# Residual stored in the output and completed by accumulating DMA in the down stage; eight VectorE sums moved one tile later

## The chip, the cores and the metric

One core of a Trainium2 chip. The metric is device time in microseconds (us) of the whole program; smaller is better. All executions told here count as fast, and the granted TensorE clock of a profiled one is given where it was not 1.0 (within 0.001). Engines: PE is TensorE's matmuls, PEld its weight loads, DVE is VectorE, ACT is ScalarE, POOL is GpSimd, SP is SyncE, which here issues DMAs only.

## The reference

```python
x = A_x                                             # 2048 x 1024, bf16
h = x + _A_ref(_layernorm(x, axis=-1), A_wqkv, A_wo)        # linear attention, 32 heads
h2 = h + _B_ref(_layernorm(h, axis=-1), B_W_gate, B_W_up, B_W_down)   # gated ReLU, F = 3584
```

`h` is needed twice: normalized for the second half, and as the residual added to the result. The second half's product is small beside it: the norm of h2 - h is 0.0023 of the norm of h2. The comparison with the reference therefore says little of the down product.

## The kernel before

Every large product is done by a scheme with seven block products in place of eight (operands are sums of blocks, made on VectorE). The program runs through k/v products, the q products and attention (to about 288 us), the gate and up products (288 to 602 us), and the down product (602 us to the end). Three parts matter here.

(1) The end of the attention stage, per tile `t` of 128 tokens. The residual `x` is loaded into `x_res` (three buffers), the attention product is added to it on VectorE, and the result `h` is stored to DRAM and normalized. Tiles 0 to 7 of `order` are processed while the last q products run, tiles 8 to 15 while the first gate/up products run:

```python
def x_in():
    x_sb = bwork.tile([P, D], BF16, tag="x_res", bufs=XB, name="x_res")        # XB = 3
    nc.sync.dma_start(out=x_sb[:], in_=xf[t * P:(t + 1) * P, :])
...
def wo_h(borrow):
    ...
    for j in range(2):
        ...   # 8 matmuls into ps ("attn")
        with tc.high_priority():
            added[t] = nc.vector.scalar_tensor_tensor(out=h_sb[:, j * NW:(j + 1) * NW], in0=ps[:], ...)
    nc.sync.dma_start(out=h_dram[i][s][:, r // P, :], in_=h_sb[:])
    ...   # ScalarE: square, Ln, Exp, normalize -> hn
def hn_T():
    nc.sync.dma_start_transpose(out=hnT[s][i][:, :, r:r + P], in_=st["hn"][:])
```

(2) VectorE is the place of several other things at that time: `phi_end` of the last q products, and the weight sums (tg, tu) of the first gate/up products, whose place is given by a scheduling constraint.

```python
def phi_end(dst, e):
    nc.scalar.activation(out=e, in_=dst, func=ACT.Exp, bias=negb[:, 0:1], scale=1.0)
    nc.vector.tensor_scalar(out=e, in0=e, scalar1=1.0, scalar2=PHI_EPS, op0=ALU.min, op1=ALU.add)   # the clamp
    nc.vector.tensor_tensor(out=dst, in0=dst, in1=e, op=ALU.max)
...
with tc.issue_after(added[order[STS - 1]].ins):     # STS = 8: after tile 7's last add
    late_sums.pop()()                               # 4 sums tg, 4 sums tu
```

(3) The down stage. The output has four quadrants (token half i, column half j). `put` finishes a piece of one: VectorE adds the accumulator and a partial result, adds `h` (loaded again from DRAM), and ScalarE's queue stores it:

```python
def load_h(k, s):
    if k in outs:
        i, j = outs[k]
        v = dpool.tile([P, NT, DW], BF16, tag="h", bufs=3, name="h")
        nc.scalar.dma_start(out=v[:], in_=h_dram[i][s][:, :, j * DW:(j + 1) * DW])
        hres[k, s] = v

def put(k, s, ts, cs, ps, m, with_h=True, eng=nc.scalar):
    ...
    add(out=ov, in0=ps, in1=m, op=ALU.add)
    if with_h:
        add(out=ov, in0=ov, in1=hres[k, s][:, ts, cs], op=ALU.add)
    t0 = (i * HS + s * SW) // P
    eng.dma_start(out=out_v[:, t0 + ts.start:..., j * DW + cs.start:...], in_=ov)
```

Of the kernel before, what the change touches and what calls it, by code (L numbers as in the profile page):

```python
# [8 lines left out]
ALU = mybir.AluOpType  # L9
FP32 = mybir.dt.float32  # L10
BF16 = mybir.dt.bfloat16
# [20 lines left out]
def block_kernel(ctx: ExitStack, tc: tile.TileContext, x, wqkv, wo, wg, wu, wd, out, H: int):  # L32
    nc = tc.nc
    P = 128
    xf = x.flatten_outer_dims()
    of = out.flatten_outer_dims()
    S, D = xf.shape
# [6 lines left out]
    NW = 512  # L44
    NDW = P + HPC
    SW = 512
    NS = S // (2 * SW)
    KH = KC // 2
    FH = FC // 2
    HS = S // 2  # L50
    NT = SW // P
    DW = D // 2
# [15 lines left out]
    nc.gpsimd.memset(deps[:], DEN_EPS)  # L68

    dram = ctx.enter_context(tc.tile_pool(name="dram", bufs=1, space=bass.MemoryType.DRAM))  # L70
    h_dram = [[dram.tile([P, NT, D], BF16, name=f"h_dram{i}_{s}") for s in range(NS)] for i in range(2)]
    GP = 2
    NE = 2 * GP
    FQ = FH // 2
# [146 lines left out]
    order = [(i * HS + s * SW) // P + tt for s in range(NS) for i in range(2) for tt in range(NT)]  # L221
# [6 lines left out]
    with ExitStack() as actx:  # L228
# [208 lines left out]
        for c in range(KC):  # L437
            bnk, i = divmod(c, GPB)
# [72 lines left out]
    held, added, squared = [], {}, {}  # L511

    def attn_stages(t):

        i, r = divmod(t * P, HS)
        s, r = divmod(r, SW)
        st = {}

        def nd():
            o_sb = bwork.tile([P, D], BF16, tag="o_sb", name="o_sb")  # L520
            st["o"] = o_sb
            held.append(o_sb)
            ov = o_sb[:].rearrange("p (k h e) -> p k h e", k=KC, h=HPC)
            for c0, n in pieces:
                ps = ndpool.tile([P, NW], FP32, tag="ab", name="nd")
                for c in range(c0, c0 + n):
                    nc.tensor.matmul(ps[:, (c - c0) * NDW:(c - c0 + 1) * NDW], lhsT=pqT[:, c, t * P:(t + 1) * P],
                                     rhs=kvz[:, c, :], start=True, stop=True)
                ndv = ps[:, 0:n * NDW].rearrange("p (k w) -> p k w", w=NDW)
                den = bsmall.tile([P, GPB, HPC], FP32, tag="den", name="den")  # L530
                nc.scalar.activation(out=den[:, 0:n], in_=ndv[:, :, P:NDW], func=ACT.Ln, bias=deps[:], scale=1.0)
                rd = bsmall.tile([P, GPB, HPC], FP32, tag="rd", name="rd")
                nc.scalar.activation(out=rd[:, 0:n], in_=den[:, 0:n], func=ACT.Exp, scale=-1.0)  # L533
                nc.vector.tensor_tensor(  # L534
                    out=ov[:, c0:c0 + n], in0=ndv[:, :, 0:P].rearrange("p k (h e) -> p k h e", h=HPC),
                    in1=rd[:, 0:n, :].unsqueeze(3).to_broadcast([P, n, HPC, Dh]), op=ALU.mult)

        def oT():
            oT = bwork.tile([P, D], BF16, tag="oT", bufs=XB, name="oT")
            st["oT"] = oT[:].rearrange("p (c t) -> p c t", c=KC)  # L540
            nc.sync.dma_start_transpose(out=st["oT"], in_=st["o"][:])

        def x_in():
            x_sb = bwork.tile([P, D], BF16, tag="x_res", bufs=XB, name="x_res")
            nc.sync.dma_start(out=x_sb[:], in_=xf[t * P:(t + 1) * P, :])
            st["x"] = x_sb

        def wo_h(borrow):
            h_sb = st["x"]
            tot = bsmall.tile([P, 2], FP32, tag="tot", name="tot")  # L550
            for j in range(2):
                if borrow:
                    ps = pspool.tile([P, NW], FP32, tag="E", bufs=2, name="attn")
                else:
                    ps = abpool.tile([P, NW], FP32, tag="ab", name="attn")
                for c in range(KC):
                    nc.tensor.matmul(ps[:], lhsT=st["oT"][:, c, :], rhs=wo_sb[:, c, j * NW:(j + 1) * NW],  # L557
                                     start=(c == 0), stop=(c == KC - 1))
                with tc.high_priority():
                    added[t] = nc.vector.scalar_tensor_tensor(out=h_sb[:, j * NW:(j + 1) * NW], in0=ps[:], scalar=1.0,  # L560
                                                   in1=h_sb[:, j * NW:(j + 1) * NW], op0=ALU.mult, op1=ALU.add,
                                                   accum_out=tot[:, j:j + 1])
            nc.sync.dma_start(out=h_dram[i][s][:, r // P, :], in_=h_sb[:])
            st["hn"] = bwork.tile([P, D], BF16, tag="hn", bufs=HB, name="hn")

            sm = bsmall.tile([P, 6], FP32, tag="sm", name="sm")
            nmean, var, lnv, rstd, nmr = (sm[:, i:i + 1] for i in range(5))
            nc.vector.tensor_scalar(out=nmean, in0=tot[:, 0:1], scalar1=tot[:, 1:2], scalar2=-1.0 / D,
                                    op0=ALU.add, op1=ALU.mult)
            squared[t] = nc.scalar.activation(out=st["hn"][:], in_=h_sb[:], func=ACT.Square, bias=nmean, scale=1.0, accum_out=var)  # L570
            nc.scalar.activation(out=lnv, in_=var, func=ACT.Ln, bias=LN_EPS, scale=1.0 / D)
            nc.scalar.activation(out=rstd, in_=lnv, func=ACT.Exp, scale=-0.5)
            nc.scalar.activation(out=nmr, in_=nmean, func=ACT.Identity, scale=rstd)
            nc.scalar.activation(out=st["hn"][:], in_=h_sb[:], func=ACT.Identity, bias=nmr, scale=rstd)

        def hn_T():
            nc.sync.dma_start_transpose(out=hnT[s][i][:, :, r:r + P], in_=st["hn"][:])

        return nd, oT, x_in, wo_h, hn_T

    LAG = (0, 1, 1, 2, 4)
    STS = ST // NS
# [4 lines left out]
    def attn_step(step):  # L587
        for k in range(len(LAG)):
            n = step - LAG[k]
            if n in begin_at:  # L590
                n = begin_at.index(n)
                if k == 3:
                    stages[n][k](QSTEPS <= step < STS + LAG[-1])
                else:
                    stages[n][k]()
                if k == len(LAG) - 1 and n % STS >= NT:
                    left_sums(hnT[n // STS], hns[n // STS], slice(n % NT * P, (n % NT + 1) * P), nc.vector)
# [177 lines left out]
    for step in range(QSTEPS + 2, ready):  # L775
        if step == QSTEPS + 2:
            flow.pop(0)()
        attn_step(step)
    with tc.issue_after(added[order[STS - 1]].ins):
        late_sums.pop()()  # L780
    steps = QSTEPS + STS + LAG[-1] - ready
    for n in range(steps):
# [19 lines left out]
    def acc(tag):  # L802
        return accs.tile([P, 2 * NW], FP32, tag=tag, bufs=2 if tag == "A" else 1, name="acc" + tag)
# [59 lines left out]
    OUTER = (1, 2, 6, 5, 3, 7, 4)  # L863
    INNER = (2, 6, 5, 3, 4)
    outs = {2: (0, 0), 7: (1, 1), 3: (0, 1), 4: (1, 0)}
# [56 lines left out]
    prv, k = None, 0  # L922
    for r, (wt, f, fi, toks) in enumerate(runs):
        w = [ops() for _, ops in now]
        later = []
        for n, s in enumerate(toks):
# [51 lines left out]
            if k == nwin - 3:  # L978
                for x in range(2):
                    t = wpools[1].tile([P, KC * 2 * GP * P], BF16, tag=("wg", "wu")[x], name="wd")  # L980
# [16 lines left out]
    for n in range(2):  # L997
        t = fpool.tile([P, 4 * D], BF16, tag="wraw", bufs=2, name="xd")
# [19 lines left out]
    dpool = ctx.enter_context(tc.tile_pool(name="dpool", **reuse))  # L1018
# [89 lines left out]
    out_v = of.rearrange("(t p) d -> p t d", p=P)  # L1108
    hres = {}

    def load_h(k, s):

        if k in outs:
            i, j = outs[k]
            v = dpool.tile([P, NT, DW], BF16, tag="h", bufs=3, name="h")
            nc.scalar.dma_start(out=v[:], in_=h_dram[i][s][:, :, j * DW:(j + 1) * DW])
            hres[k, s] = v

    def put(k, s, ts, cs, ps, m, with_h=True, eng=nc.scalar):

        i, j = outs[k]
        o = dpool.tile([P, NT * HW], BF16, tag="o", bufs=4, name="o")
        ov = o[:, 0:(ts.stop - ts.start) * (cs.stop - cs.start)].rearrange("p (t d) -> p t d", t=ts.stop - ts.start)
        add(out=ov, in0=ps, in1=m, op=ALU.add)
        if with_h:
            add(out=ov, in0=ov, in1=hres[k, s][:, ts, cs], op=ALU.add)
        t0 = (i * HS + s * SW) // P
        eng.dma_start(out=out_v[:, t0 + ts.start:t0 + ts.stop, j * DW + cs.start:j * DW + cs.stop], in_=ov)

    def cols(j):  # L1130
        return slice(j * HW, (j + 1) * HW)
# [111 lines left out]
    for n in range(1, len(OUTER)):  # L1243
# [73 lines left out]
        else:  # L1317
            pss = []
            for p in range(4):
                ps = acc(("A", "A", "XY"[(n + 1) % 2], "XY"[n % 2])[p])  # L1320
# [12 lines left out]
                s, t0 = divmod(2 * p, NT)  # L1333
                ts = slice(t0, t0 + 2)
                v = ps[:].rearrange("p (t d) -> p t d", t=2)
# [9 lines left out]
@with_exitstack  # L1345
def kernel(
    ctx: ExitStack,
    tc: tile.TileContext,
    A_x: bass.AP,
    A_wqkv: bass.AP,  # L1350
    A_wo: bass.AP,
    B_x: bass.AP,
    B_W_gate: bass.AP,
    B_W_up: bass.AP,
    B_W_down: bass.AP,
    out: bass.AP,
):
    block_kernel(tc, A_x, A_wqkv, A_wo, B_W_gate, B_W_up, B_W_down, out, H=32)
# [30 lines left out]
```

## Time and profile before

| | us |
|---|---|
| time, median of 3 runs | 738.58 (737.89 to 739.36) |
| span in the trace | 737.3 |
| PE busy | 724.7 (98%) |
| VectorE busy | 563.8 (76%) |
| PE idle between 210 and 220 us | 1.81 |

The page's first part, busy time of each engine (share of the span, count of instructions), kernel before:

```profile
PE 724.7 (98%) x4020; PEld 382.1 (52%) x4020; DVE 563.8 (76%) x992; ACT 322.4 (44%) x580; POOL 5.6 (1%) x44
```

Busy time of each engine in two stretches (stretch, its length, then busy us and instructions of PE, PEld, DVE, ACT and POOL in this order, granted clock, share of the DMA engines, GB/s):

```profile
210.00:220.00 10.00, 8.19 (x49) 4.02 (x48) 9.89 (x30) 8.55 (x28) 0.00 (x0) 1.00 0.69 129
620.00:640.00 20.00, 20.00 (x186) 17.93 (x184) 19.73 (x18) 0.00 (x0) 0.00 (x0) 1.00 0.88 315
```

From 620 to 640 us, in the down stage, PE never idles, with VectorE almost full beside it; PE has no idle time from 500 us to its last matmul. In 210 to 220 us it is VectorE that is full, and PE idles. What PE waited for in the whole run (waiting instruction, releaser: us in total, times, longest), without the waits of the first 100 us:

```profile
PE attn L557 <- DVE x_res L560: 1.3, 1, 1.3
PE attn L557 <- DVE o_sb L534: 1.1, 4, 0.5
PE nd L527 <- DVE o_sb L534: 0.5, 1, 0.5
```

VectorE's instructions in order of time there (start, length, line, output and inputs, count). L636 to L642 are the moved sums, L217 is the clamp, L560 is the add into x_res; the one at 211.99 is tile 8's first:

```profile
208.63 0.42 DVE L636 TENSOR_TENSOR tg<-wg 128x512 f16<-128x512 bf16 x1
208.97 0.42 DVE L641 TENSOR_TENSOR tg<-wg 128x512 f16<-128x512 bf16 x1
...
210.98 0.42 DVE L642 TENSOR_TENSOR tg<-wg,tg 128x512 f16<-128x512 bf16 x1
211.32 0.42 DVE L636 TENSOR_TENSOR tu<-wu 128x512 f16<-128x512 bf16 x1
211.65 0.42 DVE L217 TENSOR_SCALAR e<-e 128x1024 bf16<-128x1024 bf16 x1
211.99 0.68 DVE L560 SCALAR_TENSOR_TENSOR x_res<-attn,x_res 128x512 bf16<-128x512 f32 x1
```

And ScalarE's exponential that the clamp at 211.65 reads. It ends at 211.08:

```profile
209.94 1.14 ACT L216 ACTIVATE e<-pq_mem,negb 128x1024 bf16<-128x1024 bf16 x1
```

### The profile page before, as it was taken

How to read it: one execution, taken by the hardware profiler on the slowest of the kernel's cores; microseconds unless marked ns; L12 is line 12 of the kernel's file. 1: busy time of each engine (PE TensorE's matmuls, PEld its weight loads, DVE VectorE, ACT ScalarE, POOL GpSimd, SP SyncE). 2: the span in 40 equal slices, each digit the busy share in tenths (PEclk: the TensorE clock that was granted, in tenths of full speed). 3: DMA queues.
4: the chain of work that ended last, by engine and by line, in shares of the span. 5: the costliest groups of instructions: out<-in, count | busy, mean ns of one | idle time of the engine just before them, and what ended most of it. 6: DMA issues, size and time to landing. Idle time of an engine off the chain costs nothing.

```text
span 737.3 us, 10605 instructions
## 1 busy us (share of the span) xinstructions
PE 724.7 (98%) x4020; PEld 382.1 (52%) x4020; DVE 563.8 (76%) x992; ACT 322.4 (44%) x580; POOL 5.6 (1%) x44
## 2 busy tenths in 40 slices
PE   7999999999999999999999999999999999999997
PEld 3444555444444444444444444444444468888666
DVE  6997644677788777688768787887786379996797
ACT  4876553778887654444344444443444120000000
POOL 1000000000000000000000000000000000000000
PEclk9999999999999999999999999999999999999999
DMA  9765002079977526175638358575483499987822
GB/s 315 159 151 159 1 1 85 31 159 222 221 172 179 128 73 207 43 207 136 196 103 243 114 187 272 185 218 195 158 284 116 140 396 335 333 288 296 295 81 78
DMA packets 146594, 132.02 MB, mean 179 GB/s; under 512 B 50928, under 2 KB 128112, under 8 KB 146544
## 3 DMA queue, kind: packets, MB, share of 16 engines
q1 hardware_dynamic: 135536, 123.30, 55.8%
q10 hardware_dynamic: 11008, 8.06, 3.4%
q8 instruction: 31, 0.51, 0.3%
q14 instruction: 19, 0.16, 0.1%
HBM read 79.95 MB, written 39.85 MB: 162 GB/s over the span
## 4 chain that ended last, share of the span: by engine, by line
PE 82%; DVE 8%; DMA 5%; ACT 4%; issue 1%; SPq 0%; DVEq 0%; POOL 0%; ACTq 0%
PE accA L828 22%; PE accY L828 8%; PE accX L828 8%; PE accA L1160 8%; PE attn L557 5%; PE Aq L314 3%; PE accA L989 3%; PE accX L1160 3%; PE Aq L454 3%; PE accY L1160 2%; PE Aq L729 2%; PE Eq L314 2%; PE accY L989 2%; PE accX L989 2%; PE Eq L454 1%; PE Eq L729 1%
## 5 line engine op out<-in xcount | busy, mean ns | idle before, releaser
L838 ACT ACTIVATE gu<-gu 128x512 bf16<-128x512 bf16 x72 | 45.4, 630 | 131.2 <-DVE gu L837 131.2
L833 ACT COPY snap<-accA 128x1024 f32<-128x1024 f32 x72 | 72.5, 1008 | 36.5 <-PE accA L828 36.4
L557 PE MATMUL attn<-wo_mem,oT 128*128 128x512 bf16 x256 | 58.7, 379 | 2.7 <-DVE x_res L560 1.3
L828 PEld LDWEIGHTS <-tu 128*128 128x128 f16 x384 | 37.6, 98 | 45.3
L828 PEld LDWEIGHTS <-tg 128*128 128x128 f16 x384 | 37.6, 98 | 45.3
L837 DVE TENSOR_TENSOR gu<-accY,snap 128x1024 bf16<-128x1024 f32 x36 | 43.9, 1219 | 10.0 <-ACT snap L833 10.0
L828 PE MATMUL accA<-hn,tg 128*128 128x512 f16 (+1 forms) x192 | 49.3, 379 | 0.0
L828 PE MATMUL accA<-hn,tu 128*128 128x512 f16 (+1 forms) x192 | 49.3, 379 | 0.0
L837 DVE TENSOR_TENSOR gu<-accX,snap 128x1024 bf16<-128x1024 f32 x36 | 43.9, 1219 | 6.4 <-PE accX L828 3.7
L154 ACT COPY u<-Aq 128x512 f32<-128x512 f32 x54 | 31.3, 582 | 36.0 <-PE Aq L314 19.3
L1160 PEld LDWEIGHTS <-x 128*128 128x128 f16 (+1 forms) x448 | 43.9, 98 | 5.5
L828 PEld LDWEIGHTS <-wu 128*128 128x128 bf16 x288 | 28.2, 98 | 34.0
L828 PEld LDWEIGHTS <-wg 128*128 128x128 bf16 x288 | 28.2, 98 | 34.0
L557 PEld LDWEIGHTS <-oT 128*128 128x128 bf16 x256 | 24.7, 98 | 33.0 <-issue 4.9
L841 DVE TENSOR_TENSOR hq<-gu 128x512 bf16<-128x512 bf16 x48 | 20.3, 423 | 14.3 <-ACT gu L838 14.2
L314 PEld LDWEIGHTS <-xT 128*128 128x128 bf16 (+1 forms) x192 | 18.6, 98 | 23.7 <-issue 2.3
L534 DVE TENSOR_TENSOR o_sb<-nd,rd 128x384 bf16<-128x384 f32 (+1 forms) x48 | 23.2, 508 | 8.8 <-ACT rd L533 6.6
L1160 PEld LDWEIGHTS <-xs 128*128 128x128 f16 x280 | 27.4, 98 | 3.2
L560 DVE SCALAR_TENSOR_TENSOR x_res<-attn,x_res 128x512 bf16<-128x512 f32 x32 | 22.0, 686 | 8.4 <-PE attn L557 8.2
L989 PEld LDWEIGHTS <-x 128*128 128x128 bf16 (+1 forms) x168 | 16.4, 98 | 19.6
L1166 DVE TENSOR_TENSOR snap<-accA,u 128x1024 f32<-128x1024 f32 x16 | 19.5, 1220 | 8.3 <-PE accA L1160 8.1
L828 PE MATMUL accA<-hs,tg 128*128 128x512 f16 x96 | 24.6, 379 | 0.0
(234 smaller groups left out, 1406.1 us busy)
## 6 DMA issues: line engine op xcount, KB each, us to landing
x<-x_dram SPq DMA_DIRECT2D x17, 896.0 KB, 8.3
x_dram<-hq SPq DMA_DIRECT2D x28, 512.0 KB, 3.2
wg<-in_B_W_gate_dram SPq DMA_DIRECT2D x14, 512.0 KB, 5.2
wu<-in_B_W_up_dram SPq DMA_DIRECT2D x14, 512.0 KB, 7.3
wraw<-in_B_W_down_dram SPq DMA_DIRECT2D x14, 512.0 KB, 5.0
x_dram<-hq SPq DMA_DIRECT2D x28, 256.0 KB, 2.6
t_dram<-wt SPq DMA_DIRECT2D x28, 256.0 KB, 2.2
xd<-x_dram SPq DMA_DIRECT2D x6, 896.0 KB, 7.2
```

The source lines that it names most:

```text
L154: copies[nm, v] = nc.scalar.copy(out=snaps[nm, v], in_=bank[v][:])
L314: nc.tensor.matmul(ps[:], lhsT=left[m - 1][:, kc, r + v * P:r + (v + 1) * P], rhs=right[m - 1][:, kc, :], start=(start and kc == 0), stop= ...
L454: nc.tensor.matmul(ps[:], lhsT=rq[m - 1][:, kc, (c + v) * P:(c + v + 1) * P], rhs=left[m - 1][:, kc, :], start=(start and kc == 0), stop=( ...
L534: nc.vector.tensor_tensor(out=ov[:, c0:c0 + n], in0=ndv[:, :, 0:P].rearrange("p k (h e) -> p k h e", h=HPC), in1=rd[:, 0:n, :].unsqueeze(3 ...
L557: nc.tensor.matmul(ps[:], lhsT=st["oT"][:, c, :], rhs=wo_sb[:, c, j * NW:(j + 1) * NW], start=(c == 0), stop=(c == KC - 1))
L729: nc.tensor.matmul(ps[:], lhsT=w(v, m)[:, kc, :], rhs=left[m - 1][:, kc, :], start=(start and kc == 0), stop=(kc == KH - 1), skip_group_ch ...
L828: nc.tensor.matmul(ps[:, v, :], lhsT=w[v][n - 1][:, kc, :], rhs=left[n - 1][:, kc, :], start=(t is not None and kc == 0), stop=(kc == KH - ...
L833: nc.scalar.copy(out=st[nm][:], in_=halves(st["A"]))
L837: add(out=g[:], in0=halves(st[nm]), in1=st[base][:], op=ALU.add)
L838: nc.scalar.activation(out=g[:, 0, :], in_=g[:, 0, :], func=ACT.Relu)
L989: nc.tensor.matmul(ps[:, t * NW:(t + 1) * NW], lhsT=x_tile(n, s, kh)[:, f, (t0 + t) * P:(t0 + t + 1) * P], rhs=w_tile(n, kh)[:, f, :], sta ...
L1160: nc.tensor.matmul(pv[:, tt, :], lhsT=left(m)[:, f, tt * P:(tt + 1) * P], rhs=right(m)[:, f, :], start=(t is not None and f == 0 and tt % ...
```

## The change

Its intent: relieve VectorE and the DMA queues in the down stage, by letting the DMA engines do the addition of h. `h` goes to the output itself, except the quadrant that is finished last; for the other three `put` adds its piece to DRAM with an accumulating DMA, which GpSimd issues. And the eight weight sums are to start behind tile 8's first add, which PE waits for.

```diff
-    h_dram = [[dram.tile([P, NT, D], BF16, ...) for s in range(NS)] for i in range(2)]
+    h_dram = [dram.tile([P, NT, DW], BF16, name=f"h_dram{s}") for s in range(NS)]
 ...
-                    added[t] = nc.vector.scalar_tensor_tensor(
+                    added[t, j] = nc.vector.scalar_tensor_tensor(
 ...
-            nc.sync.dma_start(out=h_dram[i][s][:, r // P, :], in_=h_sb[:])
+            if i == 0:
+                nc.sync.dma_start(out=of[t * P:(t + 1) * P, :], in_=h_sb[:])
+            else:
+                nc.sync.dma_start(out=h_dram[s][:, r // P, :], in_=h_sb[:, 0:DW])
+                nc.sync.dma_start(out=of[t * P:(t + 1) * P, DW:D], in_=h_sb[:, DW:D])
 ...
-    with tc.issue_after(added[order[STS - 1]].ins):
+    with tc.issue_after(added[order[STS], 0].ins):
         late_sums.pop()()
 ...
-        if k in outs:
-            i, j = outs[k]
-            v = dpool.tile([P, NT, DW], BF16, tag="h", bufs=3, name="h")
-            nc.scalar.dma_start(out=v[:], in_=h_dram[i][s][:, :, j * DW:(j + 1) * DW])
+        if k == OUTER[-1]:
+            v = dpool.tile([P, NT, DW], BF16, tag="h", bufs=2, name="h")
+            nc.scalar.dma_start(out=v[:], in_=h_dram[s][:])
 ...
         add(out=ov, in0=ps, in1=m, op=ALU.add)
+        dst = out_v[...]
+        if k != OUTER[-1]:
+            nc.gpsimd.dma_start(out=dst, in_=ov, accum_op=ALU.add)
+            return
         if with_h:
             add(out=ov, in0=ov, in1=hres[k, s][:, ts, cs], op=ALU.add)
-        eng.dma_start(out=out_v[...], in_=ov)
+        eng.dma_start(out=dst, in_=ov)
```

More of the change, by code (lines that the diff above doesn't have):

```diff
@@ L70, in block_kernel @@
     dram = ctx.enter_context(tc.tile_pool(name="dram", bufs=1, space=bass.MemoryType.DRAM))
-    h_dram = [[dram.tile([P, NT, D], BF16, name=f"h_dram{i}_{s}") for s in range(NS)] for i in range(2)]
+    h_dram = [dram.tile([P, NT, DW], BF16, name=f"h_dram{s}") for s in range(NS)]
     GP = 2
@@ L559, in wo_h @@
                 with tc.high_priority():
-                    added[t] = nc.vector.scalar_tensor_tensor(out=h_sb[:, j * NW:(j + 1) * NW], in0=ps[:], scalar=1.0,
+                    added[t, j] = nc.vector.scalar_tensor_tensor(out=h_sb[:, j * NW:(j + 1) * NW], in0=ps[:], scalar=1.0,
                                                    in1=h_sb[:, j * NW:(j + 1) * NW], op0=ALU.mult, op1=ALU.add,
                                                    accum_out=tot[:, j:j + 1])
-            nc.sync.dma_start(out=h_dram[i][s][:, r // P, :], in_=h_sb[:])
+            if i == 0:
[3 more added lines that the diff above has]
+                nc.sync.dma_start(out=of[t * P:(t + 1) * P, DW:D], in_=h_sb[:, DW:D])
             st["hn"] = bwork.tile([P, D], BF16, tag="hn", bufs=HB, name="hn")
@@ L1124, in put @@
         add(out=ov, in0=ps, in1=m, op=ALU.add)
+        t0 = (i * HS + s * SW) // P
+        dst = out_v[:, t0 + ts.start:t0 + ts.stop, j * DW + cs.start:j * DW + cs.stop]
+        if k != OUTER[-1]:
+            nc.gpsimd.dma_start(out=dst, in_=ov, accum_op=ALU.add)
+            return
         if with_h:
             add(out=ov, in0=ov, in1=hres[k, s][:, ts, cs], op=ALU.add)
-        t0 = (i * HS + s * SW) // P
-        eng.dma_start(out=out_v[:, t0 + ts.start:t0 + ts.stop, j * DW + cs.start:j * DW + cs.stop], in_=ov)
+        eng.dma_start(out=dst, in_=ov)
     def cols(j):
```

## The prediction

> **What bounds the kernel now.** TensorE. The busy table gives PE 724.7 us of a 737.3 us span (98%), clock 0.999. By stage (busy time in windows): from 500 us to the last matmul, at 733.4 us, PE has no idle time. DVE is busy 19.2 to 19.7 of each 20 us from 600 to 660 us, ACT hardly at all, the DMA share 0.88 to 0.99: the down stage is bound by its matmuls, with DVE and DMA close behind. PE's 12.6 us of idle time are elsewhere: about 6 us in the first 100 us, 3.9 us after the last matmul, 2.4 us between 180 and 250 us, of which 1.8 us in 210 to 220 us. There DVE is busy 9.9 of 10 us, and PE's waits name it: 1.3 us for tile 8's add into x_res, and for o_sb (1.6 us over the stage).
>
> **What the change does.**
> 1. Down stage: of 13 DVE additions of h (0.69 us each) 12 go: 8.3 us of DVE time. Six of eight loads of h (512 KB, median 9.2 us to landing) go. Twelve 256 KB stores (median 5.1 us to landing) move from ACT to GpSimd and read, add and write DRAM. Bytes cancel: 3 MB less loaded as h, 3 MB of destination read inside the stores.
> 2. Attention stage: half of the tokens store h in two DMAs instead of one: 8 more SyncE issues of about 0.4 us, on a queue that mostly waits.
> 3. The eight sums of the first early quad (0.34 us each in the stream) start after tile 8's first add instead of after tile 7's last. Before, five of them (208.6 to 211.7 us) ran ahead of that add, which started at 211.99 us though its matmuls ended near 209.6 us (half of the 3.61 us group begun at 207.78).
>
> **On the critical path.** Step 1 relieves DVE where PE does not wait for it: worth 0. Step 2: 0, within 0.3 us. Step 3 removes the 1.3 us wait and some o_sb waits, but the sums still have to run while DVE is nearly full: gain 1.2 us (0.5 to 2). The tail keeps its stores on SyncE and ACT: 0.
>
> **Risk.** The Trainium skill ("DMA: Bandwidth & Descriptors", section "SWDGE vs HWDGE vs iDMA") says that only GpSimd can accumulate by DMA, and that its software writes descriptors into SBUF, out of which VectorE's two-port modes lock it. No run here shows it yet. DVE runs long SBUF-to-SBUF sums here (2.02 us each), so stores may start late. But an o buffer is reused after four stores, at least 16 us apart in the timeline (684 to 701): trebled landing would still fit. Should the accumulates hold up x and w loads in 600 to 632 us, PE would wait; a small chance.
>
> **Prediction:** 737.5 us, 8 in 10 between 735.5 and 741. Faster by over 2%: 0.01 (all PE idle time is under 2%). Within 2%: 0.95. Slower: 0.04.
>
> **What would show it.** Right: PE idle in 210 to 220 us falls from 1.8 to below 1 us; the x_res wait leaves PE's list; DVE's total falls by about 8 us; PE stays without idle time from 600 us to its last matmul; 12 stores on GpSimd's queue land later than 5.1 us, with no DVE wait for them. Wrong: DVE waits for o buffers, PE waits for x or w loads in the down stage, or a late GpSimd store ends the span.
>
> **What would make it wrong.** Accumulating stores several times slower than plain ones, or starved by DVE; DVE slowed by GpSimd's descriptor writes; the extra stores reordering the attention stage; the moved sums delaying the first early quad.

## More of the kernel before

Landmarks for comparing runs: starts of weight loads, of which no record is missing (matmul records sometimes are). The attn group that begins at 182.54, the first load of the up stage, the first of the down stage's inner products, and the last group:

```profile
182.54 0.10 PEld L557 LDWEIGHTS <-oT 128*128 128x128 bf16 x1
...
287.62 0.74 PEld L828 LDWEIGHTS <-wg 128*128 128x128 bf16 x4
...
601.88 3.15 PEld L1160 LDWEIGHTS <-xd 128*128 128x128 bf16 x28
...
730.08 3.04 PEld L1186 LDWEIGHTS <-xd 128*128 128x128 f16 x28
```

So 105.08 us from the attn group to the up stage (105.09 before rounding), and 131.24 us from 601.88 to the end of the last group, which begins at 730.08.

## The result and the profile after

Time after: 738.25 us, median of 4 runs (737.53 to 739.01), against 738.97 for before (4 runs, 737.89 to 740.4). A ratio is the mean time of one kernel's fast runs over that of the other's of the same rounds, so it is not quite the ratio of the medians: 0.9991, 95% interval 0.9974 to 1.0009. The two profiled runs differ by 0.1 us of span (737.2 and 737.3).

The same views as before, of the kernel after. Busy time:

```profile
PE 722.7 (98%) x3967; PEld 381.8 (52%) x4020; DVE 556.0 (75%) x980; ACT 321.5 (44%) x580; POOL 20.7 (3%) x56
```

By stretch:

```profile
210.00:220.00 10.00, 8.30 (x48) 3.94 (x48) 8.96 (x26) 9.07 (x31) 0.00 (x0) 1.00 0.73 151
620.00:640.00 20.00, 20.00 (x186) 17.93 (x184) 18.64 (x15) 0.00 (x0) 3.85 (x3) 1.00 0.94 291
```

VectorE has 7.8 us less to do in all. PE's idle time in 210 to 220 us went from 1.81 to 1.70 us only. PE's waits:

```profile
PE attn L557 <- DVE o_sb L534: 1.3, 4, 0.5
...
PE attn L557 <- DVE x_res L560: 0.8, 1, 0.8
PE nd L527 <- DVE o_sb L534: 0.5, 1, 0.5
...
PE Aq L733 <- DVE tg L644: 0.4, 1, 0.4
```

The wait for the add of tile 8 is shorter, not gone, and there is a new one, for the moved sums (tg). VectorE in order of time (an entry in brackets is idle time before the instruction and what ended it; L640 and L644 are now two of the sums):

```profile
209.58 0.42 DVE L120 TENSOR_TENSOR hs<-hn,hs 128x512 f16<-128x512 bf16 x1
210.93 0.43 DVE L217 TENSOR_SCALAR e<-e 128x1024 bf16<-128x1024 bf16 x1 [0.94 <-ACT e L216]
211.28 0.69 DVE L560 SCALAR_TENSOR_TENSOR x_res<-attn,x_res 128x512 bf16<-128x512 f32 x1
...
214.95 0.42 DVE L640 TENSOR_TENSOR tg<-wg 128x512 f16<-128x512 bf16 x1
...
219.02 0.42 DVE L644 TENSOR_TENSOR tg<-wg,tg 128x512 f16<-128x512 bf16 x1
```

This is where the expected gain went. The sums are away, but the clamp (L217) still stands ahead of the add on VectorE's queue, and it cannot start before ScalarE's exponential ends. VectorE now idles 0.94 us for it: before, the sums had filled just that time. The sums run later instead, when VectorE is full, and one comes 0.4 us too late for PE. From the attn group at 182 us to the up stage, PE's waits of over 0.15 us add up to 2.05 us before and 2.10 us after: 0.52 less for tile 8's add, 0.41 more for tg, 0.16 more for o_sb near 249 us. The other o_sb waits of the list lie at 157 to 171 us, ahead of the moved sums, so that the move could not touch them.

The landmarks:

```profile
182.13 0.10 PEld L557 LDWEIGHTS <-oT 128*128 128x128 bf16 x1
...
287.70 0.75 PEld L832 LDWEIGHTS <-wg 128*128 128x128 bf16 x4
...
601.96 3.15 PEld L1167 LDWEIGHTS <-xd 128*128 128x128 bf16 x28
...
730.16 3.04 PEld L1193 LDWEIGHTS <-xd 128*128 128x128 f16 x28
```

From 601.96 to the end of the last group it is 131.24 us, as before. The attention stretch is 105.57 us, 0.48 longer than before; the waits just added up explain 0.05 us of that. The trace after is 0.41 us ahead where that stretch begins and 0.08 us behind where it ends. Being ahead is chance: the first hundreds of instructions are the same in both kernels, and a second trace of before (below) is 0.45 us ahead as well.

### The profile page after: what moved, and what is told of

It is laid out like the page before. It is cut to its first block, busy times and chain, and to the rows that moved or that the text cites. A ratio compares the mean times of both kernels' runs of the same rounds, so it can differ in the third digit from the quotient of the medians.

```text
span 737.2 us, 10549 instructions
## 1 busy us (share of the span) xinstructions
PE 722.7 (98%) x3967; PEld 381.8 (52%) x4020; DVE 556.0 (75%) x980; ACT 321.5 (44%) x580; POOL 20.7 (3%) x56
## 4 chain that ended last, share of the span: by engine, by line
PE 85%; DVE 7%; DMA 4%; ACT 3%; issue 1%; SPq 0%; DVEq 0%; POOL 0%; ACTq 0%
PE accA L832 22%; PE accX L832 8%; PE accY L832 8%; PE accA L1167 8%; PE attn L557 6%; PE Aq L733 4%; PE Aq L314 3%; PE accA L993 3%; PE accX L1167 3%; PE Aq L454 3%; PE accY L1167 2%; PE Eq L314 2%; PE accY L993 2%; PE accX L993 2%; PE Eq L733 2%; DVE stats L272 1%
## 5 line engine op out<-in xcount | busy, mean ns | idle before, releaser
L1131 POOL DMA_DIRECT2D out_dram<-o x12 | 15.2, 1265 | 508.8 <-DMA h<-h_dram 419.1
```

## The experiments

Twelve more kernels ran, four to a chip, each beside executions of before on that chip (medians 738.57, 738.97 and 739.00 us), to which its ratio refers. What their traces show, by weight-load starts: "attention" from the attn group near 182 us to the up stage, "up" from there to the down stage's first inner product, "down" from there to the start of the last weight load. The last column is VectorE's idle time for the transposed hn near 204 us, which the text comes to.

| kernel | time, median (us) | ratio to before, 95% | attention | up | down | VectorE's wait for hn |
|---|---|---|---|---|---|---|
| before | 738.97 | | 105.09 | 314.25 | 131.15 | 1.76 |
| before_again | 738.77 | 0.9994 (0.9979 to 1.0010) | 105.15 | 314.25 | 131.15 | 1.91 |
| after | 738.25 | 0.9991 (0.9974 to 1.0009) | 105.57 | 314.25 | 131.15 | 1.45 |
| after_again | 738.50 | 0.9991 (0.9976 to 1.0007) | 105.47 | 314.25 | 131.15 | 1.46 |
| edge_only | 739.17 | 1.0002 (0.9988 to 1.0017) | 105.49 | 314.25 | 131.15 | 1.81 |
| down_only | 737.57 | 0.9983 (0.9969 to 0.9997) | 104.38 | 314.25 | 131.15 | 0.83 |
| edge_fix | 740.49 | 1.0020 (1.0003 to 1.0036) | 106.54 | 314.25 | 131.15 | 1.40 |
| split_only | 738.03 | 0.9983 (0.9970 to 0.9996) | 104.23 | 314.25 | 131.15 | 0.82 |
| down_nosplit | 738.04 | 0.9986 (0.9973 to 0.9999) | 104.31 | 314.25 | 131.15 | 1.08 |
| down_split_all | 739.16 | 1.0000 (0.9987 to 1.0013) | 105.97 | 314.25 | 131.15 | 1.25 |
| down_xpool | 750.56 | 1.0158 (1.0128 to 1.0189) | 114.14 | 314.25 | 131.15 | 2.19 |
| dve_plus | 744.43 | 1.0069 (1.0046 to 1.0091) | 104.30 | 314.25 | 137.40 | 1.06 |
| acc_full_dve | 737.93 | 0.9983 (0.9970 to 0.9997) | 104.51 | 314.25 | 131.15 | 0.93 |
| gp_plain | 738.76 | 0.9993 (0.9977 to 1.0009) | 105.49 | 314.25 | 131.15 | 1.42 |

The clock was 0.995 in the traces of down_xpool and dve_plus. Ratios are of means, and in each group of 11, 11 and 9 executions of before one to three had a mean clock of 0.995 to 0.998, and were mostly the longest. With the executions below 0.999 left out on both sides, the ratios of 0.9983 to 0.9986 in the table are 0.9987 to 0.9990.

In the expectations below, stretches were read from starts of matmuls, which differ from those of the loads: 104.91 (before) and 105.40 (after) there are 105.09 and 105.57 here, and the down stage's 129.63, to an earlier end point, is 131.15 here.

### edge_only: the moved sums alone

```diff
-    with tc.issue_after(added[order[STS - 1]].ins):
+    with tc.issue_after(added[order[STS], 0].ins):
```

> The kernel before with only the sums moved behind tile 8's first add. Read on TensorE: from the 16 matmuls of attn that begin near 182.9 us to the first accA of the up stage near 287.8 us (before: 104.91 us; after the whole change: 105.40, so 0.49 longer). If the move of the sums is what costs that, this stretch is 105.4 here, within 0.1; if the split stores of h (SyncE's order) cost it, it is 104.9. The prediction's theory (the move gains 1.2 us) would have 103.7. Down stage, from the first accA inner product (602.25) to the last pair of matmuls (731.88): 129.63, as before, for every theory. Time: within 1 us of before.

Measured: attention 105.49 against 105.09, time 1.0002. PE's program order is that of after, and so are the signs of the move: VectorE idles 0.93 us for the exponential, PE waits 0.8 us for the add and 0.4 us for tg. So the move by itself brought no gain, and the stretch it was to shorten is 0.4 us longer in this trace.

### down_only: everything but the moved sums

```diff
-    with tc.issue_after(added[order[STS], 0].ins):
+    with tc.issue_after(added[order[STS - 1], 1].ins):
```

> The whole change without the moved sums (their place is that of before; TensorE's order is then the same as before). If the moved sums alone cost the 0.49 us, the stretch from the attn group near 182.9 to the first accA of the up stage is 104.9, within 0.1; if the split stores of h cost it, 105.4. Down stage 129.6 within 0.1, as in both kernels. Rival for the time: the down stage's relief is worth something in the fast runs (then below 0.998 of before); mine: 0.999 to 1.001.

Measured: the down stage as always, but attention 104.38, which neither side had expected: 0.7 shorter than before, with PE, ScalarE and VectorE there in before's order. The time, 0.9983, lies between the two forecasts (0.999 to 1.001, and below 0.998), and the rival's mechanism is out: nothing was gained in the down stage. VectorE waited 0.83 us instead of 1.76 for a transposed hn.

### edge_fix: tile 8's add ahead of the clamp

```diff
+    tc.add_manual_dep(ends[-1].ins, added[order[STS], 0].ins.name, ...NoSync..., reason="order")   # ends: the clamps
```

> The whole change, and the last query pair's clamp (which waits for ScalarE's exponential, and on VectorE stood ahead of tile 8's first add) is ordered behind that add. If the wait of 0.8 us that is left in after comes from that clamp, TensorE's wait for the add of tile 8 is gone (below 0.1) and tile 8's first add starts before 210 us instead of at 211.28. If it comes from DVE being full, it stays at 0.5 us or more. Whether the stretch from the attn group to the first accA gets shorter: mine is by 0.3 to 0.8 us against after (104.6 to 105.1); if VectorE's backlog decides, the waits come back later for o_sb and tg and it stays at 105.4.

Measured: tile 8's first add starts at 208.99 us and PE no longer waits for it, which shows that the clamp had held it. But the waits came back, and larger. PE's waits in edge_fix (its lines are shifted by two):

```profile
PE nd L529 <- DVE o_sb L536: 2.1, 2, 1.6
...
PE attn L559 <- DVE o_sb L536: 1.1, 3, 0.5
PE Eq L735 <- DVE tg L642: 1.1, 1, 1.1
```

Attention is 106.54 and the time 1.0020 of before. The second half of the expectation, a shorter stretch, was wrong. Moving the one add was not enough, but what the rest costs this run does not isolate: with the new order the scheduler also moved work on PE (from 210.8 us on) and on ScalarE (from 223 us on).

### after_again

The kernel after, unchanged.

> The whole change once more, for how well the trace repeats. The start (first 50 weight loads, to 13.5 us in after and 13.97 in before) has the same instructions in both: if it is chance, it differs here by some tenths from 13.5. The stretch from the attn group near 182.5 to the first accA: 105.4 within 0.1 if the scheduling and not chance made it longer than before; within 0.3 of 104.9 if it is chance. Time 0.998 to 1.001 of before.

Measured: 105.47, time ratio 0.9991. It repeats.

### before_again

The kernel before, unchanged.

> The kernel before once more, for how well its trace repeats: the stretch of 104.91 us in the attention stage, within 0.2 if program order decides it, and the first 50 weight loads at 13.4 to 13.6 us as in the five later traces (so that the 13.97 of the first trace was chance). Time 1.000 of before within 0.0015.

Measured: 105.15, ratio 0.9994; the start is like that of most other traces (the 50th weight load 0.57 us earlier than in the first trace of before).

### split_only and down_nosplit: how h is stored

split_only is before with this change alone:

```diff
-            nc.sync.dma_start(out=h_dram[i][s][:, r // P, :], in_=h_sb[:])
+            (i == 0: as before; i == 1:)
+                nc.sync.dma_start(out=h_dram[i][s][:, r // P, 0:DW], in_=h_sb[:, 0:DW])
+                nc.sync.dma_start(out=h_dram[i][s][:, r // P, DW:D], in_=h_sb[:, DW:D])
```

> The kernel before, with nothing but the lower half's store of h cut in two halves of 128 KB. In down_only the attention stage (from the attn group near 182 us to the first accA of the up stage) was 0.7 us shorter than in before, with TensorE's and VectorE's instructions there in the same order. If the two smaller stores do that (they land sooner: median 2.2 and 1.9 us against 3.5; the load of x_res that waits for them stands ahead of the transposes on SyncE's queue), this run shows it too: 104.2 within 0.2 and a time of 0.998 to 0.9995 of before. If it was chance in how DMAs landed, or came from where h is stored, it is 104.9 and 1.000.

Measured: 104.23 and 0.9983. This looked like the answer. down_nosplit is down_only with single stores, all to the output (the last quadrant reads its h from there):

```diff
+            nc.sync.dma_start(out=of[t * P:(t + 1) * P, :], in_=h_sb[:])
-            nc.scalar.dma_start(out=v[:], in_=h_dram[s][:])
+            nc.scalar.dma_start(out=v[:], in_=out_v[:, (HS + s * SW) // P:(HS + s * SW) // P + NT, 0:DW])
```

> down_only, with one store of h for the lower half too (all of h to the output; the last product reads its h from there). If splitting the store is what made down_only faster, the gain is gone: stretch 104.9 within 0.2, time 0.9995 to 1.001 of before. If the gain comes from the down stage or from storing into the output, it stays: 104.2, and 0.998 to 0.999.

Measured: 104.31 and 0.9986, so splitting is not needed for the gain.

### down_xpool: the loads of x_res from GpSimd

```diff
-            nc.sync.dma_start(out=x_sb[:], in_=xf[t * P:(t + 1) * P, :])     # in x_in
+            nc.gpsimd.dma_start(out=x_sb[:], in_=xf[t * P:(t + 1) * P, :])
```

> down_only, with the loads of x_res issued by GpSimd instead of SyncE, so that a load that waits for a store of h to land no longer holds up the transposes behind it. (The scheduler also moves some VectorE instructions.) If that hold-up is what decides, VectorE's waits for the transposed hn in 200 to 222 us (0.8 us in down_only, 1.8 in before) are below 0.4 and the stretch is below 104.2, the time below 0.9983 of before. If VectorE's backlog decides, the stretch stays at 104.2 or above.

Measured: 114.14 and 1.0158, far worse (in the trace partly because the granted clock was 0.50 for 3.41 us twice in this stretch, from 217.2 and from 265.0 us), and VectorE's wait for hn near 206 us is 2.19 us. The transposes of o_sb now took a median of 5.2 us to land (3.5 in down_only), the loads 4.3 (3.1), and PE waited 7.8 us in all for o_sb, gu, x_res and oT in 180 to 300 us. The scheduler had reordered several engines too, so this run does not say what the hold-up on SyncE's queue costs.

### down_split_all: the supposed best version

As in down_nosplit the last quadrant reads its h from the output; each store is cut in two:

```diff
+            for ks in (slice(0, DW), slice(DW, D)):
+                nc.sync.dma_start(out=of[t * P:(t + 1) * P, ks], in_=h_sb[:, ks])
```

> The best parts together: the down stage of the change, h of all tokens in the output, each 256 KB store of it in two halves, the sums where before has them. If an earlier landing of these stores is what shortened the attention stage (by 0.8 to 0.9 us in down_only, split_only and down_nosplit), it is shorter by 0.8 to 1.2 us here too, and the time 0.998 to 0.9988 of before. If SyncE's 16 additional issues begin to cost, the stretch is longer than in down_only.

Measured: 105.97 and 1.0000; PE waits 1.2 us for tile 8's add. The theory that smaller, earlier landing stores shorten the stretch falls here: the version with most of them is no faster than before, and down_nosplit gained without them.

### dve_plus: the removed additions doubled instead

```diff
             add(out=ov, in0=ov, in1=hres[k, s][:, ts, cs], op=ALU.add)
+            if k != OUTER[-1]:
+                add(out=ov, in0=ov, in1=hres[k, s][:, ts, cs], op=ALU.add)
```

> The kernel before, with every one of the 12 additions of h of the first three quadrants done twice (a wrong result on purpose): the cost that the change takes away, doubled. Down stage, from the first accA inner product to the start of the last matmul group on accY (before: 602.25 to 731.88, 129.63 us). If VectorE's relief is worth nothing because TensorE never waits for it, with room to spare: still 129.6, time 1.000 of before. If VectorE was at its limit (19.7 of 20 us busy in 620 to 640 us): up to 8.3 us more of VectorE's time there, and TensorE waits for snap or o: 131 or more, time above 1.002.

Measured (a wrong result): 137.40 instead of 131.15, and 1.0069. So VectorE had had too little room for this: PE now waits for it, at 638 and at 723 us. PE's new wait, and two stretches around the second of its two parts (after GpSimd's busy time come the granted clock, the share of the DMA engines and GB/s):

```profile
PE accA L1162 <- DVE snap L1168: 4.3, 2, 2.4
```

```profile
720.00:723.00 3.00, 0.62 (x6) 0.41 (x5) 2.91 (x4) 0.00 (x0) 0.00 (x0) 1.00 0.43 123
723.00:728.00 5.00, 5.00 (x32) 3.84 (x31) 3.03 (x4) 0.00 (x0) 0.00 (x0) 0.66 0.74 241
```

The waits make up 4.3 us of the 6.25. After the second one the granted clock was 0.50 for 3.41 us (0.66 is the mean of the 5 us shown), and 28 matmuls took 4.88 us where others take 3.22: another 1.7 us. That part does not come every time: the two executions with a mean clock of 1.000 took 742.42 and 743.14 us, 3.4 and 4.1 more than before's median of 739.00 there; the two at 0.995 and 0.998 took 745.72 and 745.80.

### acc_full_dve: the accumulating stores without the relief

```diff
         if k != OUTER[-1]:
+            add(out=ov, in0=ov, in1=ov, op=ALU.add)
             nc.gpsimd.dma_start(out=dst, in_=ov, accum_op=ALU.add)
```

> The whole change, with 12 additions of the same size put back on VectorE ahead of the accumulating stores (a wrong result on purpose): the cost of the new stores without the relief that came with them. If the stores cost TensorE nothing by themselves: down stage 129.6, time as after (0.999 to 1.001 of before). Rival: relief and stores cancel; then it is longer than 129.63 by what the stores cost, some tenths to some us.

Measured: down 131.15. The stores cost PE nothing even with VectorE as full as before (19.76 of 20 us in 620 to 640 us), so relief and cost did not cancel; both are worth zero. The time was 0.9983 where 0.999 to 1.001 was expected; the difference lies in the attention stretch. (It doubles part of the down product.)

This run taught something else. Its instructions on every engine are those of after, in the same order, up to the down stage, and yet the attention stretch took 104.51 us instead of 105.57. Likewise dve_plus has before's, and took 104.30 instead of 105.09. So one and the same order of instructions comes in two lengths there, about 1 us apart. In the five short traces (down_only, split_only, down_nosplit, dve_plus, acc_full_dve) VectorE waited 0.8 to 1.1 us for the transposed hn near 204 us, in all the long ones 1.25 to 2.2. Is this chance at each execution, or something fixed in a kernel? It is not shown: the five short traces are of five kernels that differ from before and after in their stores or in the down stage, and the two kernels that were traced twice agreed within 0.1 us each time (105.09 and 105.15, 105.57 and 105.47). The first four executions of after spread over 1.5 us (737.53 to 739.01), which leaves room for either.

An earlier event looks like a cause and does not hold up: the landing of the load of x_res that is issued at 186.9 to 188.8 us. It took 3.0 to 3.3 us in all five short traces and 3.9 to 6.0 us in six of the long ones (6.0 in after, 3.9 in before), but 3.1 and 3.2 us in before_again and edge_only, which were long all the same. (down_xpool, which issues it from GpSimd, is not counted.)

One step nearer to VectorE's wait the traces say more. The transpose that it waits for was issued 17.84 to 17.86 us after the attn landmark in all five short traces, and 17.98 to 18.78 us after it in the eight long ones, down_xpool again left out. On SyncE's queue it stands behind a load of x_res into a buffer whose store of h has to land first: that store landed 16.6 us after the landmark in dve_plus, but 17.7 to 17.9 us after it in before, before_again and edge_only, and the load was issued within 0.3 us of it. So a late landing of a store can hold up the transpose. Why it lands late, and so what sets the length, stays open: no run held everything but one landing fixed.

### gp_plain: plain stores from GpSimd

```diff
-            nc.gpsimd.dma_start(out=dst, in_=ov, accum_op=ALU.add)
+            nc.gpsimd.dma_start(out=dst, in_=ov)
```

> The whole change, with the 12 stores from GpSimd made plain (a wrong result on purpose). It splits the longer landing (from the start of the issue to landing, median 6.9 against 5.5 us in before): if the accumulation in DRAM makes it longer, it falls below 5.5 us here (issue still 1.2 to 1.4 us); if the issue from GpSimd does[...], it stays near 6.5. The time does not move in either case.

Measured (a wrong result). The list of DMA issues (count, size, median us from issue to landing), first after, then gp_plain:

```profile
out_dram<-o POOLq DMA_DIRECT2D x12, 256.0 KB, 6.9
```

```profile
out_dram<-o POOLq DMA_DIRECT2D x12, 256.0 KB, 5.0
```

The accumulation makes the landing, counted from the start of the issue, 1.9 us longer. The issue itself takes GpSimd 1.28 us with it and 0.75 us without (medians), so the 1.2 to 1.4 us expected for it here was a miss. Issuing from GpSimd alone does not delay landing: the same twelve stores, issued by ScalarE in before, took 5.5 us (5.1 over all 14 of this size).

## Why the prediction was right or wrong

The number was right: 737.5 us was forecast and 738.25 measured, inside the range, and "within 2%" held. But the time of before lies in that range as well, so the number does not test the steps, and that it came within 1 us of the forecast is luck: the gain was to come from step 3, and that step failed.

**What bounds the kernel: right.** PE has no idle time in the down stage in before or after, and that stage has the same length to 0.01 us.

**Step 1, worth 0: right, and shown.** VectorE's total fell by 7.8 us ("8.3 us" forecast); the down stage stayed at 131.15 us with the relief (down_only, after), without it (acc_full_dve), and without the accumulation (gp_plain). The reason "relieves DVE where PE does not wait for it" holds. It was not said, and dve_plus showed, how little room was left: the same 8.3 us added cost 6.25 us in the trace, and 3.4 and 4.1 us in the two executions without a fall of the clock. The change bought room for something later, not time now.

**Step 2, "0, within 0.3 us": open.** split_only was 0.9 us shorter in the attention stretch and 0.9983 in time, but down_split_all went the other way, and a kernel without the split (dve_plus) reached 104.30 too. The unexplained 1 us between short and long traces hides it.

**Step 3, "gain 1.2 us (0.5 to 2)": wrong, the failed step.** The sentence was "Step 3 removes the 1.3 us wait and some o_sb waits". The runs show the wait at 0.8 (0.6 in after_again), the o_sb waits no smaller (1.3 and 1.1 us, 1.1 before), and a new one of 0.4 us for tg. In acc_full_dve, which has after's order, the wait for tile 8's add is gone from the list, and still its 104.51 us are no gain on the short traces without moved sums (104.23 to 104.38), with o_sb at 1.3 us and tg at 0.4. Among the long traces the move alone gave 105.49 us against 105.09 and 105.15 (edge_only, before, before_again), and after, after_again and gp_plain took 105.47 to 105.57. So in no pair does the gain of 0.5 to 2 us appear. How large a loss stands in its place is not shown: down_split_all, without moved sums, took 105.97. The misreading: that five sums ran ahead of the add was taken as their delaying it, by over 2 us (from 209.6 to 211.99). Between them and the add stood the clamp, and the exponential that it waits for ended at 211.08. Only the 0.57 us from there to the clamp's start at 211.65 can be due to the sums. That the clamp held the add, edge_fix shows.

**The small difference of the medians** (0.72 us the first time, 0.07 the second time) is not shown to be a gain. The two first traces are only 0.1 us apart: a start that happened to be 0.4 us earlier, 0.48 us lost in the attention stage, and 0.2 us less from the last weight load to the end (4.32 to 4.12). The last is found in every trace with the changed down stage (4.11 to 4.14 against 4.29 to 4.32); its cause was not looked for, and the forecast had "The tail ... 0".

**What would show it.** Came true: PE without idle time from 600 us on, the GpSimd stores landing later than 5.1 us in the median (6.9; four of the twelve took 4.1 to 4.7), no VectorE wait for an o buffer. Did not: idle time in 210 to 220 us below 1 us (1.70), the x_res wait gone. On the risk: the Trainium skill ("DMA: Bandwidth & Descriptors", section "SWDGE vs HWDGE vs iDMA") says that VectorE's two-port modes lock GpSimd out of the memory its descriptors go to. No run here shows it: plain stores issued by GpSimd beside VectorE's long sums landed in 5.0 us; in which mode those sums ran the trace does not tell, so this is no test of it.

Of all versions down_only has the lowest median, 737.57 us; its ratio of 0.9983 it shares with split_only and acc_full_dve. The lead of these rests on the attention stretch, whose length differs by 1 us for one order of instructions without a known cause, and it is under 0.2%.

## What to carry to other kernels

Before moving work out from in front of an instruction that is waited for, look at what else stands ahead of it on the same queue and when that could have started at the earliest; work that fills a forced wait costs nothing, and moved away it must be paid for elsewhere. Taking work off an engine that the bounding engine does not wait for gives no time, however full it looks: what it gives is room, and doubling the work is a quick way of measuring how much there was. Cut two traces at landmarks that both have before believing a difference of some tenths in the total, and run each kernel's trace twice: here the start alone moved by 0.57 us between two traces of the same kernel, more than any of the parts that were compared.

## What the Trainium skill lacked or had wrong

- "DMA: Bandwidth & Descriptors" says that accumulation is for GpSimd to issue, but not its cost. Here, for 256 KB stores: issue 1.28 us against 0.75 us plain, landing 6.9 us against 5.0 us (medians of 12).
- "TensorE: Matmul & The Clock Gate" (section "Part 1: The HAM clock gate (the "warmup" mystery)") has the clock fall after at least one idle window of about 3.4 us. In dve_plus a wait of 2.38 us was enough: PE was busy for 1.03 of the 3.41 us before the fall, and the granted clock was then 0.50 for 3.41 us. A wait of 1.88 us in the same run was not followed by any fall.
- No page says how far the length of a stretch with many small DMAs can differ for one and the same order of instructions: here by about 1 us in 105 between kernels that differ elsewhere (105.57 and 104.51), and by 0.1 us or less between two traces of one kernel.
